# A fused attention, dense and expert kernel: another order of the work around the routing of tokens and between the two stages

## The chip, the cores and the metric

The kernel runs on one core of one Trainium2 chip. The metric is the device time of one execution in microseconds (us). Before the change the median of three runs is 1416.9 us (1415.62 to 1420.39). TensorE appears as PE, VectorE as DVE, ScalarE as ACT, GpSimd as POOL, and SyncE, which issues the transfers, as SP.

## What is computed

Attention in chunks of 64 gives x for 4608 tokens of 512 numbers. A dense layer with a parametric ReLU follows, and on its result a mixture of eight experts, of which each token takes one (cut from the reference):

```python
h = x @ w_in                                              # (4608, 2048)
g = np.maximum(h, 0.0) + alpha * np.minimum(h, 0.0)
x = g @ w_out                                             # (4608, 512)
logits = x @ w_gate                                       # 8 experts
expert_idx = np.argmax(logits, axis=1)
...
gate_w = probs[np.arange(N), expert_idx]                  # softmax weight of that expert
for e in range(E):
    mask = expert_idx == e
    out[mask] = gate_w[mask, None] * (np.maximum(x[mask] @ w1[e], 0.0) @ w2[e])   # 512 -> 1024 -> 512
```

## The kernel before

**Numbers.** Each float32 operand of a large matmul is split into a high and a low part, and three matmuls stand for one product. The high part is an ACT copy, the low part a subtraction, mostly on POOL.

**Dense stage.** The 36 tiles of 128 tokens go in 18 pairs j, each pair in 16 steps m of 128 hidden units, step s = 16 j + m in all. In a step TensorE does mm1 (12 matmuls, L328), ACT takes the positive and the negative part from PSUM (g_r, L344 and L345), DVE joins them with alpha (g_x, L350), ACT and POOL split the result (g_h L354, g_l L358), and TensorE accumulates mm2 (6 matmuls, L380) three steps behind mm1 into the banks y0 and y1, one for each tile of the pair. There are two buffers r, so the Relu of step s waits until g_l of step s - 2 has read its own. Every step also carries pieces of the attention of later tiles (exponentials px, their row sums sr, the product L269 on POOL, the transpose ptt L274 on DVE, matmuls L186 and L299) and of the split of the expert weights (ACT L467, POOL L468), which SP writes to HBM and later loads in blocks of 2 MB, the ring.

**Routing of a tile.** When a pair is done, gate_ev copies its two banks into rows (ACT L392), which sets y0 and y1 free for the next pair. Then gate_l makes eight dot products on DVE (L404), gate_a the largest logit and the one-hot tile oh (DVE L413 to L419), gate_e the exponential (ACT L425), gate_r the rank of each token among those of its expert (two small matmuls, L435 reading oh and L436 reading the running sum ohsum), gate_b weight, place and the new ohsum (DVE L450 to L458) and an indirect scatter of the row into the experts' table in HBM (POOL L459).

**Order.** It is written out by hand. The dictionaries pre and bg hold what a step does besides its own work; GATE (L558) sets the steps of a tile's routing, counted from the start of the pair behind its own: pieces of gate_l, then (a, r, b), the steps of gate_a, gate_r and gate_b. Even and odd tiles have different rows. Each engine works through its instructions in the order of the program:

```python
hooks(pre, s); g_b(*order[s - 1]); mm1(j, m); g_a(j, m); hooks(bg, s)
while done <= s - 3: mm2(*order[done]); done += 1
```

**Expert stage.** The expert tokens come in slots t of 128 rows. load gets them, with an address from a table, in transfers on SP's queue, tx transposes and splits them (blocks: DVE L661, ACT L663, POOL L664), m1(t, f) does 12 matmuls of 512 columns for one half f of the hidden units and 16 copies hx out of PSUM (ACT L692 or DVE L694), th(t, f) transposes and splits these, m2(t, f) does 12 matmuls more. Slots 0 to 3 (FULL is 4) use an expert that was picked before all counts were known; from slot 4 on addresses and weights come from tables that DVE computes from the counts of all tiles (table_count to table_refill). load_early fetches the second half of the ring, refill the blocks after it, under flags that table_refill writes. A value that SP or TensorE has to read holds up all that stands behind it on that queue.

**Between the stages** stands the tuple START (L885): the routing of the last two tiles a and b, the slots 0 to 3 and the tables, in one order by hand. It ends with tx(5) and table_refill, and the loop behind it goes over t from 3 on: tx(t + 2), m1(t + 1, 0), refill, m1(t + 1, 1), refill, th(t + 1), m2(t, 0), m2(t, 1), load(t + 4).

Of the kernel before, what the change touches and what calls it, by code (L numbers as in the profile page):

```python
# [42 lines left out]
def tile_attention_moe(ctx, tc, q, k, v, w_in, w_out, alpha, w_gate, w1, w2, out):  # L43
    nc = tc.nc
    NB = q.shape[0]
    NTILE = 2 * NB
    FULL = (NTILE - 4) // 8
    NT = 128 * NTILE
    MF = 16
# [7 lines left out]
    T = NTILE + 2 * (E - 1)  # L57
    TS = NTILE + 3
# [475 lines left out]
    def at(step, f, *args):  # L534
        bg.setdefault(step, []).append((f, args))
# [12 lines left out]
    for i in range(4):  # L548
        for d, e0, f in GATE0[i]:
# [12 lines left out]
    )  # L562
    for i in range(4, NTILE - 2):
        s0 = MF * (i // 2 + 1)
        pre.setdefault(s0 + 3, []).append((gate_ev, (i,)))
        *parts, (a, r, b) = GATE[2 if i % 2 and i >= NTILE - 5 else i % 2]
        for d, e0, e1 in parts:
            at(s0 + d, gate_l, i, e0, e1)
        at(s0 + a, gate_a, i)
        at(s0 + a + 1, gate_e, i)  # L570
        at(s0 + r, gate_r, i)
        pre.setdefault(s0 + b, []).append((gate_b, (i,)))
# [109 lines left out]
    def m1(t, f):  # L682
        if f == 0 and t >= FULL:
            half[t] = nc.tensor.value_load(rt[0:1, 0, t:t + 1], min_val=0, max_val=1)
        p = hbank("h", 3)
        passes(p, xT[t], f, t, True, True)
        hx[t, f] = P2["hx"].tile([128, 4, 128], F32, name="hx")
        for I in range(4):
            for J in range(4):
                src, dst = p[32 * I:32 * I + 32, 128 * J:128 * J + 128], hx[t, f][32 * J:32 * J + 32, I]  # L690
                if f == 0 or t < FULL:
                    nc.scalar.activation(out=dst, in_=src, func=ACTF.Relu)  # L692
                else:
# [185 lines left out]
    for t in range(3):  # L879
# [3 lines left out]
    at(B0 + 9, tx, 1)  # L883
    a, b = NTILE - 2, NTILE - 1
    START = (  # L885
        (mm2, NB - 1, MF - 1), (gate_ev, a), (gate_ev, b), (gate_l, a, 0, 4), (m1, 0, 0), (gate_l, a, 4, 8),
        (m1, 0, 1), (gate_a, a), (th, 0, 0), (gate_l, b, 0, 1), (gate_e, a),
        (m1, 1, 0), (th, 0, 1), (tx, 2), (gate_l, b, 1, 4), (gate_r, a), (m1, 1, 1), (th, 1, 0), (gate_b, a),
        (load_early, 1, 0), (gate_l, b, 4, 8), (gate_a, b), (gate_e, b), (m2, 0, 0), (load_early, 1, 1), (m2, 0, 1),
        (tx, 3), (m1, 2, 0), (th, 1, 1), (table_count,), (gate_r, b), (gate_b, b), (m1, 2, 1), (table_experts,),  # L890
        (th, 2, 0), (load_early, 1, 2), (m2, 1, 0), (table_places,), (table_own, 0, 8), (table_base, 0, 8), (load, 4),
        (load, 5), (m2, 1, 1), (th, 2, 1),
        (m1, 3, 0), (table_own, 8, T), (table_order,), (th, 3, 0), (tx, 4), (m1, 3, 1), (load_early, 1, 3), (th, 3, 1),
        (table_next,), (m2, 2, 0), (table_base, 8, T), (m2, 2, 1), (load, 6), (tx, 5), (table_refill,),
    )

    def hooks(d, s):
        for f, args in d.pop(s, []):
            f(*args)

    with tc.manual_schedule():
# [40 lines left out]
        mm2(j, m - 1)  # L942
        for f, *args in START:
            f(*args)
        for t in range(3, TS):
            more, two, dyn = t + 1 < TS, t + 2 < TS, t >= FULL
            if two and t > 3: tx(t + 2)
            if more: m1(t + 1, 0)
            if dyn: refill(t, 0)
            if more: m1(t + 1, 1)  # L950
            if dyn: refill(t, 1)
            if more:
                th(t + 1, 0)
# [66 lines left out]
```

## Time and profile before

| | |
|---|---|
| runs, median (lowest to highest) | 1416.9 us (1415.62 to 1420.39) |
| profiled execution, its own time | 1414.75 us |
| its span | 1412.9 us |
| mean granted TensorE clock | 0.989 |
| busy: PE, DVE, ACT, POOL | 1336.7, 1039.9, 825.5, 741.0 us |
| attention and dense stage | to about 950 us of the span |
| between the stages, up to m1(6, 0) | 949.80 to 1027.70 us |

A row of a timeline gives the start in us from the begin of the span, the length of the instruction (or of several, xN), engine, line, operation, output and inputs, and in brackets how long the engine sat idle before it and what ended that. Busy times of matmuls overlap a little, since they are pipelined.

### The profile page before, as it was taken

What the parts mean: (1) busy time and instruction counts of PE and PEld (TensorE: products, weight loads), DVE (VectorE), ACT (ScalarE), POOL (GpSimd) and SP (SyncE); (2) the same over time, 40 slices, a digit from 0 to 9 for tenths busy, and PEclk for the clock granted to TensorE, in tenths of its full rate; (3) what the DMA queues carried; (4) which work ended last, traced back from release to release, by engine and by line L of the source; (5) the groups of instructions that cost most, each with busy time, mean ns of one, the idle gap of its engine ahead of it and who ended that gap; (6) DMA issues with size and microseconds to landing.
All of it is one profiled execution on the core that took longest, in us unless ns stands there. A gap on an engine that the chain in (4) does not pass through costs nothing. (4 is left out here: it accounts for less than half of the span.)

```text
span 1412.9 us, 31146 instructions
## 1 busy us (share of the span) xinstructions
PE 1336.7 (95%) x9515; PEld 1155.7 (82%) x9515; DVE 1039.9 (74%) x2510; ACT 825.5 (58%) x2297; POOL 741.0 (52%) x754
## 2 busy tenths in 40 slices
PE   7788999999999999999999999998899999999997
PEld 6667888889888888988888898886688888878775
DVE  7996789788788778878877887567756556655553
ACT  4555555656556565655656565438565666556553
POOL 4553467665666666566666654333344444444443
PEclk9999999999999999999999999999999999999999
DMA  6645445655555555555555551191324415865543
GB/s 230 201 151 183 153 165 197 200 179 188 182 188 184 195 193 178 190 182 192 180 196 191 179 182 46 39 389 74 118 55 165 165 50 214 329 240 219 182 170 140
DMA packets 107306, 249.16 MB, mean 176 GB/s; under 512 B 15552, under 2 KB 36544, under 8 KB 103040
## 3 DMA queue, kind: packets, MB, share of 16 engines
q1 hardware_dynamic: 101136, 227.37, 47.6%
q0 software_dynamic: 6000, 19.70, 3.7%
q8 instruction: 84, 1.38, 0.4%
q14 instruction: 86, 0.70, 0.2%
HBM read 401.39 MB, written 88.91 MB: 347 GB/s over the span
## 5 line engine op out<-in xcount | busy, mean ns | idle before, releaser
L328 PEld LDWEIGHTS h<-xt,ring 128*128 128x128 f32 x3456 | 456.4, 193 | 40.3 <-DVE xt L315 4.0
L328 PE MATMUL h<-xt,ring 128*128 128x256 f32 x3456 | 466.1, 285 | 13.0 <-DVE xt L315 3.5
L380 PE MATMUL y<-ring,g 128*128 128x512 f32 x1728 | 457.0, 400 | 5.4 <-POOL g L358 3.0
L380 PEld LDWEIGHTS y<-ring,g 128*128 128x128 f32 x1728 | 307.1, 190 | 62.6 <-POOL g L358 4.7
L358 POOL TENSOR_TENSOR g<-r,g 128x256 fp32r<-128x256 f32 x281 | 248.4, 887 | 130.6 <-ACT g L354 113.4
L404 DVE CUSTOM_DVE_ANT_0 junk<-row,wgb 128x512 bf16<-128x512 f32 x288 | 268.9, 934 | 7.7 <-ACT row L392 3.6
L468 POOL TENSOR_TENSOR sp<-eraw,sp 128x512 fp32r<-128x512 f32 x128 | 177.9, 1390 | 162.2 <-ACT sp L467 136.4
L694 DVE TENSOR_SCALAR hx<-h 32x128 f32<-32x128 f32 x560 | 160.7, 287 | 104.6 <-PE h L676 97.4
L676 PE MATMUL y<-ring,hT 128*128 (+1 forms) x936 | 225.0, 395 | 10.4 <-ACT hT L663 7.2
L664 POOL TENSOR_TENSOR hT<-z,hT 128x512 fp32r<-128x512 f32 x78 | 100.2, 1303 | 253.4 <-ACT hT L663 250.2
L676 PE MATMUL h<-ring,xT 128*128 (+1 forms) x936 | 226.5, 396 | 5.2 <-DMA ring<-wsp 3.7
L676 PEld LDWEIGHTS y<-ring,hT 128*128 128x128 f32 x936 | 177.0, 190 | 52.7 <-ACT hT L663 9.3
L344 ACT ACTIVATE r<-h 128x256 f32<-128x256 f32 x288 | 110.3, 383 | 185.0 <-PE h L328 93.2
L676 PEld LDWEIGHTS h<-ring,xT 128*128 128x128 f32 x936 | 175.7, 188 | 48.9 <-ACT xT L663 4.0
L354 ACT ACTIVATE g<-r 128x256 fp32r<-128x256 f32 x288 | 119.3, 414 | 149.4 <-DVE r L350 79.3
L692 ACT ACTIVATE hx<-h 32x128 f32<-32x128 f32 x688 | 184.4, 268 | 10.6 <-PE h L676 3.0
L663 ACT ACTIVATE hT<-z 128x512 fp32r<-128x512 f32 x78 | 47.9, 633 | 123.6 <-DVE z L661 122.6
L257 ACT ACTIVATE px<-s 32x256 f32<-32x256 f32 x240 | 89.9, 375 | 4.1 <-DVE s L246 1.2
L467 ACT ACTIVATE sp<-eraw 128x512 fp32r<-128x512 f32 x128 | 80.8, 631 | 1.0
L661 DVE STREAM_TRANSPOSE z<-xg 128x512 f32<-128x512 f32 x39 | 27.7, 710 | 50.4 <-POOL hT L664 50.4
L661 DVE STREAM_TRANSPOSE z<-hx 128x512 f32<-128x512 f32 x78 | 51.3, 692 | 13.7 <-ACT hx L692 10.1
L664 POOL TENSOR_TENSOR xT<-z,xT 128x512 fp32r<-128x512 f32 x39 | 51.7, 1325 | 11.9 <-ACT xT L663 11.5
(734 smaller groups left out, 1192.9 us busy)
## 6 DMA issues: line engine op xcount, KB each, us to landing
ring<-wsp SPq DMA_DIRECT2D x148, 2048.0 KB
wsp<-sp SPq DMA_DIRECT2D x128, 512.0 KB
eraw<-in_w SPq DMA_DIRECT2D x128, 256.0 KB
xg<-xs SPq DMA_DIRECT2D x156, 64.0 KB
vt<-in_v SPq DMA_DIRECT2D x18, 512.0 KB
qt<-in_q SPq DMA_DIRECT2D x17, 512.0 KB
kt<-in_k SPq DMA_DIRECT2D x17, 512.0 KB
iraw<-in_w_in SPq DMA_DIRECT2D x16, 512.0 KB
```

What stands on the lines that cost most here:

```text
L257: nc.scalar.activation(out=p[J:J + 32, t], in_=s[I:I + 32, e], func=ACTF.Exp, scale=scale)
L328: nc.tensor.matmul(out=h, lhsT=w[:, wl, a, 128 * mi:128 * mi + 128], rhs=x[:, xl, a], start=(n == 0), stop=(n == 11),)
L344: nc.scalar.activation(out=r, in_=h, func=ACTF.Relu)
L354: nc.scalar.activation(out=gs[j, m][:, 0], in_=rs[j, m][0], func=ACTF.Copy)
L358: eng.tensor_tensor(out=g[:, 1], in0=r, in1=g[:, 0].bitcast(F32), op=ALU.subtract)
L380: nc.tensor.matmul(out=ys[j][t], lhsT=g[:, gl, 128 * t:128 * t + 128], rhs=w[:, wl, mi], start=(m == 0 and n == 0), stop=(m == MF - 1 and ...
L404: nc.vector.tensor_tensor_reduce(out=junk, in0=r[:, 0:512], in1=wgb[e // 2][:, e % 2], scale=1.0, scalar=0.0, op0=ALU.mult, op1=ALU.add, a ...
L468: eng.tensor_tensor(out=dst[:, 1], in0=raw, in1=dst[:, 0].bitcast(F32), op=ALU.subtract)
L664: nc.gpsimd.tensor_tensor(out=dst[:, 1], in0=z, in1=dst[:, 0].bitcast(F32), op=ALU.subtract)
L676: ins.append(nc.tensor.matmul(out=out, lhsT=lhs[:, xl, a], rhs=w[:, rows_, wl, a], start=(first and a == 0 and n == 0), stop=(last and a = ...
L692: nc.scalar.activation(out=dst, in_=src, func=ACTF.Relu)
L694: V.tensor_scalar(out=dst, in0=src, scalar1=0.0, scalar2=None, op0=ALU.max)
```

## The change

Three things. **GATE:** for tiles 4 to 29 the odd row's (a, r, b) goes from (16, 17, 18) to (17, 22, 24): gate_a one step later, the rank matmuls five steps behind it, gate_b two steps behind these. The even row's gate_b goes from step 15 to 16. Tiles 30 to 33 keep what they had. **hx:** the 16 copies of m1(3, 1) go from ACT to DVE (`t < FULL - 1`). **START:** rewritten, and extended to m2(4, 1); the loop begins at slot 5. In the new file, lines behind L563 have a number higher by one, and those behind START one lower by three.

```diff
     GATE = (
+        ((3, 0, 2), (4, 2, 3), (5, 3, 4), (6, 4, 6), (8, 6, 8), (9, 14, 16)),
+        ((10, 0, 2), (11, 2, 4), (12, 4, 5), (13, 5, 6), (14, 6, 8), (17, 22, 24)),
         ((3, 0, 2), (4, 2, 3), (5, 3, 4), (6, 4, 6), (8, 6, 8), (9, 14, 15)),
-        ((10, 0, 2), (11, 2, 4), (12, 4, 5), (13, 5, 6), (14, 6, 8), (16, 17, 18)),
         ((11, 0, 2), (12, 2, 5), (13, 5, 8), (13, 15, 16)),
     )
...
-        *parts, (a, r, b) = GATE[2 if i % 2 and i >= NTILE - 5 else i % 2]
+        *parts, (a, r, b) = GATE[i % 2 + (2 if i >= NTILE - 6 else 0)]
...
-                if f == 0 or t < FULL:
+                if f == 0 or t < FULL - 1:
...
-        (load_early, 1, 0), (gate_l, b, 4, 8), (gate_a, b), (gate_e, b), (m2, 0, 0), (load_early, 1, 1), (m2, 0, 1),
...
+        (m2, 0, 0), (load_early, 1, 1), (gate_r, b), (th, 1, 0), (table_count,), (table_experts,), (gate_e, b),
...
+        (table_base, 8, T), (m2, 3, 0), (th, 4, 1), (load, 7), (table_refill,), (m1, 5, 0), (refill, 4, 0), (load, 8),
+        (m2, 3, 1), (th, 5, 0), (m1, 5, 1), (refill, 4, 1), (m2, 4, 0), (th, 5, 1), (m2, 4, 1),
     )
+    FIRST = 5
...
-        for t in range(3, TS):
+        for t in range(FIRST, TS):
             more, two, dyn = t + 1 < TS, t + 2 < TS, t >= FULL
-            if two and t > 3: tx(t + 2)
+            if two: tx(t + 2)
```

TensorE in the dense stage, at the end of a pair (y_6936 and y_6937 are its banks). Before:

```order
L328 MATMUL h<-xt,ring_65 128x256 x12
L435 LDWEIGHTS tri
L435 MATMUL rk<-oh,tri 128x8
L436 LDWEIGHTS ones
L436 MATMUL rk<-ohsum,ones 128x8
L380 MATMUL y_6936<-ring_68,g 128x512 x3
L380 MATMUL y_6937<-ring_68,g 128x512 x3
L328 MATMUL h<-xt,ring_65 128x256 x12
L380 MATMUL y_6936<-ring_68,g 128x512 x3
L380 MATMUL y_6937<-ring_68,g 128x512 x3
L328 MATMUL h<-xt,ring_65 128x256 x12
```

The odd tile's rank matmuls (L435, L436) stand here two steps ahead of the pair's last mm2. After, at the begin of the next pair, whose banks are y_7625 and y_7626:

```order
L380 MATMUL y_7625<-ring_66,g 128x512 x3
L380 MATMUL y_7626<-ring_66,g 128x512 x3
L328 MATMUL h<-xt,ring_67 128x256 x12
L380 MATMUL y_7625<-ring_66,g 128x512 x3
L380 MATMUL y_7626<-ring_66,g 128x512 x3
L328 MATMUL h<-xt,ring_67 128x256 x12
L435 LDWEIGHTS tri
L435 MATMUL rk<-oh,tri 128x8
L436 LDWEIGHTS ones
L436 MATMUL rk<-ohsum,ones 128x8
L380 MATMUL y_7625<-ring_66,g 128x512 x3
L380 MATMUL y_7626<-ring_66,g 128x512 x3
```

Now the old pair closes without them, and they stand after the third mm2 of the new pair.

ACT at the same place, where the two L392 are the evictions of the pair's banks. Before:

```order
L344 ACTIVATE r<-h 128x256
L345 ACTIVATE n__7506<-h 128x256
L425 ACTIVATE lg,se<-lg 128x8
L467 ACTIVATE sp<-eraw 128x512
L354 ACTIVATE g<-r 128x256
L344 ACTIVATE r<-h 128x256
L345 ACTIVATE n__7554<-h 128x256
L392 ACTIVATE row<-y_6936 128x512
L392 ACTIVATE row<-y_6937 128x512
L354 ACTIVATE g<-r 128x256
```

After:

```order
L344 ACTIVATE r<-h 128x256
L345 ACTIVATE n__7496<-h 128x256
L467 ACTIVATE sp<-eraw 128x512
L354 ACTIVATE g<-r 128x256
L344 ACTIVATE r<-h 128x256
L345 ACTIVATE n__7541<-h 128x256
L425 ACTIVATE lg,se<-lg 128x8
L392 ACTIVATE row<-y_6924 128x512
L392 ACTIVATE row<-y_6925 128x512
L354 ACTIVATE g<-r 128x256
```

The exponential of the odd tile (L425) went behind the parts of one more step and is the last instruction ahead of the evictions.

POOL there (L459 is the scatter of a tile's rows, L269 the product of the attention). Before:

```order
L468 TENSOR_TENSOR sp<-eraw,sp 128x512
L459 DMA xs<-row,posi 36864x514
L358 TENSOR_TENSOR g<-r,g 128x256
L269 TENSOR_TENSOR px<-px,sr 128x512
L468 TENSOR_TENSOR sp<-eraw,sp 128x512
L358 TENSOR_TENSOR g<-r,g 128x256 x2
L468 TENSOR_TENSOR sp<-eraw,sp 128x512
L459 DMA xs<-row,posi 36864x514
L358 TENSOR_TENSOR g<-r,g 128x256
L393 COPY row<-toki 128x1 x2
```

After:

```order
L468 TENSOR_TENSOR sp<-eraw,sp 128x512
L358 TENSOR_TENSOR g<-r,g 128x256
L269 TENSOR_TENSOR px<-px,sr 128x512
L468 TENSOR_TENSOR sp<-eraw,sp 128x512
L459 DMA xs<-row,posi 36864x514
L358 TENSOR_TENSOR g<-r,g 128x256 x2
L468 TENSOR_TENSOR sp<-eraw,sp 128x512
L358 TENSOR_TENSOR g<-r,g 128x256
L393 COPY row<-toki 128x1 x2
L358 TENSOR_TENSOR g<-r,g 128x256
```

The even tile's scatter went from ahead of L269 to behind it and the split L468, ahead of the two g_l of steps 15 and 16; the odd tile's left this place for the next pair's steps.

TensorE between the stages, from m1(1, 1) on (h is an output of m1, y one of m2). Before:

```order
L676 MATMUL h<-ring_66,xT 128x512 x12
L676 MATMUL y<-ring_67,hT 128x512 x12
L676 MATMUL y<-ring_68,hT 128x512 x12
L676 MATMUL h<-ring_65,xT 128x512 x12
L725 LDWEIGHTS ones
L725 MATMUL cps<-ohsum,ones 128x8
L726 LDWEIGHTS ones
L726 MATMUL cps<-oh,ones 128x8
L435 LDWEIGHTS tri
L435 MATMUL rk<-oh,tri 128x8
L436 LDWEIGHTS ones
```

After:

```order
L677 MATMUL h<-ring_66,xT 128x512 x12
L677 MATMUL y<-ring_67,hT 128x512 x12
L435 LDWEIGHTS tri
L435 MATMUL rk<-oh,tri 128x8
L436 LDWEIGHTS ones
L436 MATMUL rk<-ohsum,ones 128x8
L726 LDWEIGHTS ones
L726 MATMUL cps<-ohsum,ones 128x8
L727 LDWEIGHTS ones
L727 MATMUL cps<-oh,ones 128x8
L677 MATMUL h<-ring_65,xT 128x512 x12
L677 MATMUL y<-ring_68,hT 128x512 x12
```

Between m2(0, 0) and m2(0, 1) stand now the last tile's rank, the count (L726, L727) and m1(2, 0); the rank stood behind m1(2, 0) and the count before it.

## Rows read from the trace of the kernel before

**Rows 1.** The page's part 1, the busy times of the engines.

```profile
PE 1336.7 (95%) x9515; PEld 1155.7 (82%) x9515; DVE 1039.9 (74%) x2510; ACT 825.5 (58%) x2297; POOL 741.0 (52%) x754
```

**Rows 2.** Waits of TensorE: released tile, releaser, total us, times, longest.

```profile
PE rk L435 <- DVE oh L418: 17.2, 13, 1.4
```

**Rows 3.** Timeline of TensorE, the end of one pair: start, length, operation, idle before.

```profile
596.28 1.59 PE L328 MATMUL h<-xt,ring 128*128 128x256 f32 x12
597.71 0.18 PE L435 MATMUL rk<-oh,tri 128*128 128x8 f16 x1
...
604.90 1.59 PE L328 MATMUL h<-xt,ring 128*128 128x256 f32 x12
607.82 0.17 PE L435 MATMUL rk<-oh,tri 128*128 128x8 f16 x1 [1.32 <-DVE oh L418]
...
614.77 1.43 PE L380 MATMUL y<-ring,g 128*128 128x512 f32 x5
```

**Rows 4.** Timeline of DVE, same stretch.

```profile
602.17 0.47 DVE L350 SCALAR_TENSOR_TENSOR r<-n__8127,nalpha,r 128x256 f32<-128x256 f32 x1
...
605.52 0.15 DVE L413 TENSOR_REDUCE gmx<-lg 128x1 f32<-128x8 f32 x1
...
607.68 0.77 DVE L419 TENSOR_SCALAR lg<-lg,gmx 128x8 f32<-128x8 f32 x1
...
610.25 0.11 DVE L450 TENSOR_SCALAR se<-se 128x1 f32<-128x1 f32 x1
```

**Rows 5.** Timeline of POOL, same stretch.

```profile
602.38 1.17 POOL L459 DMA_INDIRECT xs<-row,posi  x1 [0.15 <-ACT sp L467]
...
605.31 1.20 POOL L269 TENSOR_TENSOR px<-px,sr 128x512 f32<-128x512 f32 x1 [0.98 <-DVE sr L268]
606.47 1.26 POOL L468 TENSOR_TENSOR sp<-eraw,sp 128x512 fp32r<-128x512 f32 x1
607.70 1.43 POOL L358 TENSOR_TENSOR g<-r,g 128x256 fp32r<-128x256 f32 x2
```

**Rows 6.** Timeline of ACT, same stretch.

```profile
601.47 0.38 ACT L345 ACTIVATE n__8127<-h 128x256 f32<-128x256 f32 x1
...
608.46 0.39 ACT L344 ACTIVATE r<-h 128x256 f32<-128x256 f32 x1 [2.34 <-POOL g L358]
...
609.00 0.21 ACT L425 ACTIVATE lg<-lg 128x8 f32<-128x8 f32 x1
...
611.66 1.29 ACT L392 ACTIVATE row<-y 128x512 f32<-128x512 f32 x2
```

**Rows 7.** Timeline of DVE behind the dense stage: dot products and gate_a of tile a.

```profile
949.95 0.69 DVE L404 CUSTOM_DVE_ANT_0 junk<-row,wgb 128x512 bf16<-128x512 f32 x1 [3.58 <-ACT row L392]
...
955.84 0.16 DVE L413 TENSOR_REDUCE gmx<-lg 128x1 f32<-128x8 f32 x1
...
956.63 0.23 DVE L419 TENSOR_SCALAR lg<-lg,gmx 128x8 f32<-128x8 f32 x1
```

**Rows 8.** Timeline of TensorE between dense and expert stage.

```profile
962.49 0.73 PE L676 MATMUL y<-ring,hT 128*128 128x512 f32 x2 [1.18 <-ACT hT L663]
...
969.20 4.06 PE L676 MATMUL y<-ring,hT 128*128 128x512 f32 x10 [0.64 <-POOL hT L664]
...
1019.60 0.73 PE L676 MATMUL y<-ring,hT 128*128 x2 [3.53 <-ACT hT L663]
```

**Rows 9.** Windows: stretch, busy time of each engine (count), granted clock, DMA share.

```profile
949.80:1027.70 77.90, 67.50 (x271) 51.02 (x270) 59.03 (x184) 55.88 (x186) 25.93 (x21) 0.96 0.33 112
1027.70:1105.27 77.57, 77.57 (x338) 63.23 (x337) 45.90 (x133) 47.00 (x140) 34.22 (x28) 1.00 0.40 136
```

**Rows 10.** Groups of TensorE from 949.8 to 1027.7: busy, mean ns, idle before.

```profile
L676 PE MATMUL h<-ring,xT 128*128 128x512 f32 (+1 forms) x144 | 35.6, 399 | 1.5 <-POOL xT L664 1.5
L676 PE MATMUL y<-ring,hT 128*128 128x512 f32 (+1 forms) x120 | 33.2, 429 | 8.9 <-ACT hT L663 6.4 <-POOL hT L664 2.5
```

**Rows 11.** The page's part 5, the hx copies on DVE.

```profile
L694 DVE TENSOR_SCALAR hx<-h 32x128 f32<-32x128 f32 x560 | 160.7, 287 | 104.6 <-PE h L676 97.4
```

More of the change, by code (lines that the diff above doesn't have):

```diff
@@ L885, in tile_attention_moe @@
     START = (
-        (mm2, NB - 1, MF - 1), (gate_ev, a), (gate_ev, b), (gate_l, a, 0, 4), (m1, 0, 0), (gate_l, a, 4, 8),
-        (m1, 0, 1), (gate_a, a), (th, 0, 0), (gate_l, b, 0, 1), (gate_e, a),
-        (m1, 1, 0), (th, 0, 1), (tx, 2), (gate_l, b, 1, 4), (gate_r, a), (m1, 1, 1), (th, 1, 0), (gate_b, a),
-        (load_early, 1, 0), (gate_l, b, 4, 8), (gate_a, b), (gate_e, b), (m2, 0, 0), (load_early, 1, 1), (m2, 0, 1),
[L890 to L894, printed above, removed]
+        (mm2, NB - 1, MF - 1), (gate_ev, a), (gate_l, a, 0, 4), (gate_ev, b), (gate_l, a, 4, 8), (gate_l, b, 0, 1),
+        (gate_a, a), (m1, 0, 0), (m1, 0, 1), (th, 0, 0), (gate_e, a), (tx, 2), (gate_l, b, 1, 4), (gate_l, b, 4, 8),
+        (m1, 1, 0), (load_early, 1, 0), (gate_r, a), (gate_b, a), (gate_a, b), (th, 0, 1), (m1, 1, 1), (tx, 3),
+        (m2, 0, 0), (load_early, 1, 1), (gate_r, b), (th, 1, 0), (table_count,), (table_experts,), (gate_e, b),
+        (m1, 2, 0), (gate_b, b), (th, 1, 1), (m2, 0, 1), (load_early, 1, 2), (table_places,), (m1, 2, 1),
+        (load_early, 1, 3), (table_own, 0, 8), (table_base, 0, 8), (th, 2, 0), (table_own, 8, T), (th, 2, 1), (load, 4),
+        (tx, 4), (m1, 3, 0), (table_order,), (m2, 1, 0), (m1, 3, 1), (m2, 1, 1), (load, 5), (m2, 2, 0), (th, 3, 0),
+        (tx, 5), (m2, 2, 1), (table_next,), (load, 6), (th, 3, 1), (m1, 4, 0), (m1, 4, 1), (tx, 6), (th, 4, 0),
+        (table_base, 8, T), (m2, 3, 0), (th, 4, 1), (load, 7), (table_refill,), (m1, 5, 0), (refill, 4, 0), (load, 8),
+        (m2, 3, 1), (th, 5, 0), (m1, 5, 1), (refill, 4, 1), (m2, 4, 0), (th, 5, 1), (m2, 4, 1),
     )
+    FIRST = 5
     def hooks(d, s):
```

## The prediction

> **What bounds the kernel now.** I read four views in this order. First the page's busy times: TensorE works in 1336.7 of the span's 1412.9 us, 95% [rows 1], so a gain has to come out of the some 76 us in which it doesn't, and any other engine matters only where TensorE waits for it. Second, TensorE's waits: the longest entry is the rank matmul of a token tile waiting for its one-hot tile, 17.2 us in 13 waits [rows 2]. Third, the timeline of TensorE over the end of one pair of tiles, where that wait is seen twice: the even tile's rank matmul starts 1.43 us after the mm1 before it (596.28 to 597.71, no wait), the odd tile's 2.92 us after it (604.90 to 607.82) [rows 3]. Fourth, the stretch between dense and expert stage, 949.80 to 1027.70. It holds 264 expert matmuls (144 with output h, 120 with output y), ahead of which TensorE sat idle for 1.5 and 8.9 us [rows 10]. In the steady expert stage behind it 338 matmuls take 77.57 us, 0.2295 us each [rows 9].
>
> The profiled execution took 1414.75 us (span 1412.9); the sum is made against it. The median of the runs is 1416.9, 2.15 higher, and I add that at the end. About 0.3%, 4.3 us, is what a measurement of this kernel tells from no change.
>
> **The rank matmuls (GATE).** For 13 odd tiles the step of the rank matmul moves from one behind the one-hot tile to five behind it. A step is one mm1 and one mm2, close to 2.9 us, so the matmul comes some 14 us after the one-hot and cannot wait for it. Removed: 2.92 - 1.43 = 1.49 us per pair, 13 x 1.49 = 19.4 us (the waits alone, 17.2, leave out the refilling of the pipe). The 13 even tiles keep their rank matmul at step 14 and only move their bookkeeping and scatter by a step. Nothing is added: the same matmuls, DVE instructions and scatters are issued.
>
> What is late next? The one-hot piece (gate_a) of the odd tile is now one step later on DVE, and its exponential stands on ACT directly ahead of the two evictions that set the y banks free for the next pair. TensorE's first mm2 of that pair began at 614.77 [rows 3] and now wants its bank 1.49 earlier, at 613.28. I follow the chain to the eviction with the old durations:
> - ACT's negative part of step 15 starts at 601.47 and takes 0.38 [rows 6], so DVE's g_x can start at about 601.85. It stood at 602.17 behind the even tile's gate_b [rows 4], which has gone from there, so everything from it to POOL's px moves 0.3 earlier: px from 605.31 [rows 5] to 605.0.
> - POOL then does px (1.16 to the next start), the split sp (1.23), and now the even tile's scatter, which stood ahead of px at 602.38: 1.35 with the gap before it. Then g_l of step 15, 0.72, half of the pair at 607.70 [rows 5]. It will end at 609.5 (605.0 + 1.16 + 1.23 + 1.35 + 0.72), where it ends at 608.4 now.
> - ACT's Relu of step 17 waits for exactly that (608.46, after 2.34 us idle) [rows 6]. From there over the negative part, DVE's g_x and the transpose ptt to the next DVE instruction at 610.25 [rows 4] are 1.79 us, so gate_a starts at about 611.3.
> - gate_a costs 1.0 us undisturbed (955.84 to 956.86) [rows 7] and 2.9 at this place now (605.52 to 608.45) [rows 4]. Then 0.2 for the exponential and 0.64 for one eviction [rows 6]. So y0 comes free between 613.1 and 615.0: margin from +0.1 to -1.8 us.
>
> The difference is what POOL does meanwhile. At 605.5 POOL ran a split and two g_l back to back; at 611.3 I expect the end of a split and one g_l, so one held instruction and not three: 1.0 + 0.5 (half of a POOL instruction of 0.72 to 1.3 us) = 1.5. That frees the bank at 613.64, 0.36 late; 13 x 0.36 = 4.7 us. **Dense stage: 4.7 - 19.4 = -14.7 us**, with ends -19.4 (no new wait) and 13 x 1.76 - 19.4 = +3.5 (a new wait of 1.76 each time).
>
> That DVE's small instructions stretch beside POOL is in the rows: the same lg instruction takes 0.23 in one place and 0.77 in the other [rows 4, 7]. The Trainium skill, "SBUF — State Buffer", section "Who interferes with whom", says that DVE and GpSimd share one port pair under an exclusive lock, and that a DVE instruction with two SBUF inputs is held by a GpSimd instruction that reads SBUF until that has ended. By that rule gate_a's cost depends on where POOL's instructions fall, and a placement like today's gives the +3.5 end, a sum of -8; by my reading of POOL's order it is -14.7.
>
> **The transition (START).** 264 x 0.2295 = 60.6 us of matmuls stand in 77.9, so 17.3 us are lost there: 10.4 idle [rows 10], about 0.04 x 67.5 = 2.7 from a granted clock that averages 0.96 where the steady stage has 1.00 [rows 9] (of the two levels, 1.2 and 2.4 GHz, it shows the lower in part of it, behind waits), the remaining 4.2 refilling after each wait. In the new order other blocks stand between a transpose and its reader. I go through the waits:
> - m2(0,0) still comes right behind m1(1,1), four blocks after the start, and th(0,0) still stands behind 32 hx copies on ACT. The wait stays: 1.18 for ACT and about 0.64 for POOL [rows 8], 1.8. If the clock falls behind it, ten matmuls that need 2.3 at full pace took 4.06 [rows 8], up to 1.8 more; I take 1.0.
> - m2(0,1) gets m1(2,0) ahead of it (12 x 0.23 = 2.8) and m2(1,1) gets m1(3,1): their waits go. m2(4,0) waited 3.53 [rows 8], because hx(4,1) stood behind the whole of table_refill on DVE. Now it stands ahead of it, and m2(3,0), m1(5,0), m2(3,1), m1(5,1), 11 us, lie between m1(4,1) and m2(4,0). Gone, with the slow clock behind it.
> - New: the last tile's rank matmul stands right behind m2(0,0), at 949.8 + 60 x 0.23 + 1.8 = 965.4 or a little later. Its one-hot on DVE: 16 dot products at 0.74 (949.95 to 955.84 for eight [rows 7]), two gate_a at 1.0, and two transposes and a gate_b, 0.7 each by their lengths in this stretch: 15.9 in all, 965.8. From 0 to 2.3 (with one gate_a at 2.9 instead of 1.0); I take 1.0. Its matmuls and the count's hold everything behind them on TensorE.
> - New: m1(6,0) waits for refill(4,0) on SP's queue, which waits for the flags at the end of table_refill. DVE had 59.0 us of work in the stretch [rows 9], of which about 6 come behind the flags; 16 hx copies of slot 3 come to it (16 x 0.287 = 4.6) [rows 11]. About 58 of the 66 us that would be left: free if DVE idles under 8 us before that. It idled 18.9 in the whole stretch now. From 0 to 3; I take 0.5. SP's skipped transfers themselves cost nothing that TensorE sees.
> - The 16 copies leave ACT, which is not last there any more; on DVE m2(1,1) and m2(2,0), 5.5 us, cover their 4.6. All ring loads of half 1 go ahead of load(4) now; what a late xT costs TensorE is 1.5 us in the whole stretch now [rows 10]: nothing taken, half of it at the upper end.
> - Refilling: I leave two fifths of the 4.2, 1.7, for the first wait and the two that can be new.
>
> What stays is 1.8 + 1.0 + 1.0 + 0.5 + 1.7 = 6.0: **transition 17.3 - 6.0 = -11.3 us**. Ends: -14.7, where only the first wait and half of that refilling stay (1.8 + 0.8 = 2.6 of 17.3), and -5.9, where everything stands at its upper end (1.8 + 1.8 + 2.3 + 3 + 1.7 + 0.8 = 11.4).
>
> **Sum.** -14.7 - 11.3 = -26 us: 1388.75 on the profiled execution, 1390.9 against the median. I say 1391. The slots behind m2(4,1) are the same as before and steady.
>
> **Rivals.**
> - *Nothing takes the place.* For it: the bank's margin is +0.1 with an undisturbed gate_a, and DVE and POOL may run earlier than I chain them. Against it: every number of the chain would have to be at its low end. -19.4 - 14.7 = -34.1: 1382.8. Chance 0.14.
> - *The eviction waits at its far end.* gate_a is held as long as now, in all 13 pairs: dense +3.5, transition -11.3, together -8: 1409; half way, 1401. For it: the 2.9 at today's place [rows 4]. Against it: POOL's order behind that g_l is lighter there. 0.14, for times from 1401 to 1413.
> - *Slower, by the same bank.* If one more POOL split (1.23) gets ahead of g_l of step 15, the bank comes 1.76 + 1.23 = 2.99 late: 13 x (2.99 - 1.49) = +19.5 in the dense stage, less 11.3, +8: 1425. For it: POOL has a split in most steps, and one that is issued a step early blocks g_l for its whole length [rows 5]. Against it: the new order of POOL shows none there. It decides from 1.49 + 11.3 / 13 = 2.36 us late, 0.6 beyond the far end of my chain. 0.04.
> - *The change doesn't do what it says*: a rank matmul could still wait, now for the sum of one-hots (ohsum) that the even tile's later gate_b writes. Against it: that gate_b stands ahead of the odd tile's gate_a on DVE, so it is done five steps before as well. Then only the transition gains, 1405.6, or with its waits moved to loads behind SP's queue nothing, 1417. Together 0.06.
>
> **How the numbers follow.** My forecast, a gain of 16 to 32 us, has 0.62, times from 1385 to 1401. The time I give is its sum, 1391. The range 1382 to 1406 takes in the first rival and the lower half of the second, and leaves out some 0.17. Faster by over 0.3%: 0.62 + 0.14 + 0.13 + 0.03 = 0.92; within 0.3%: 0.04; slower: 0.04.
>
> **What would show it.** The waits of TensorE should have no "rk <- DVE oh" of 13 times any more; a new entry of a dense y (L380) waiting for an ACT row (L392) with 13 times and 0.2 to 0.6 us each is my term of 4.7, about none the first rival, 1.8 each the second. Between the first m1(0,0) and m1(6,0) should lie about 66.6 us, with the wait of m2(0,0) unchanged, none for hT of slot 4, and at most 1 to 2 us for the last rank matmul. I am wrong in the mechanism if the dense stage gains less than 8 us without that y wait, or if the transition gains under 6.

## The result, and the profile after

The changed kernel takes 1400.05 us (median of four runs, 1399.02 to 1401.04), the kernel before beside it 1418.64 (1415.62 to 1421.03): a ratio of 0.987, 95% interval 0.9846 to 0.9894. The forecast was faster, 1391 us, in a range from 1382 to 1406. The direction and the range held; the time lies 9 us above the forecast, and the profile shows that this is not noise but a step of the working.

The profiled execution took 1399.97 us, its span is 1398.2, 14.7 less than before. Four places of it answer to the rows above. First the waits of TensorE over the whole span (released tile, releaser, total us, times, longest), the two longest and the one for the flags, and then the one for the ring in the kernel before:

```profile
PE h L677 <- DMA ring<-wsp: 8.0, 5, 3.3
PE rk L435 <- DVE xt L315: 6.7, 13, 3.2
...
PE h L677 <- DVE cm L853: 1.5, 1, 1.5
```

```profile
PE h L676 <- DMA ring<-wsp: 3.7, 3, 1.6
```

The 17.2 us for the one-hot tile [rows 2] are gone. In their place the rank matmul waits for xt, the DVE instruction that reads the attention's product o (one of the 13 waits, 3.2 us, is in the kernel before as well), and the waits for the ring are now the largest entry.

Second, TensorE at an even tile's rank matmul (590.40, step 14 as before), at the first mm2 of the next pair (605.83), and at the odd tile's rank matmul (614.39), which stands behind the third mm2 of that pair, against [rows 3]:

```profile
588.53 1.59 PE L328 MATMUL h<-xt,ring 128*128 128x256 f32 x12
590.40 0.18 PE L435 MATMUL rk<-oh,tri 128*128 128x8 f16 x1 [0.28 <-DVE xt L315]
...
605.83 1.66 PE L380 MATMUL y<-ring,g 128*128 128x512 f32 x6
...
612.96 1.59 PE L328 MATMUL h<-xt,ring 128*128 128x256 f32 x12
614.39 0.18 PE L435 MATMUL rk<-oh,tri 128*128 128x8 f16 x1
```

The odd tile's matmul follows its mm1 at 1.43 us, where it was 2.92: all of the 1.49 is gone. But the even tile's, which was not moved, now follows its mm1 at 1.87 us with a wait, where it was 1.43 without one. So 0.44 a pair have come in at a place that the change doesn't name.

Third, the stretch between the stages. It was 77.90 us from the first m1 to m1(6,0) [rows 9]; now:

```profile
936.10 8.56 PE L677 MATMUL h<-ring,xT 128*128 128x512 f32 x36
...
948.79 0.73 PE L677 MATMUL y<-ring,hT 128*128 128x512 f32 x2 [1.18 <-ACT hT L664]
950.52 2.58 PE L677 MATMUL y<-ring,hT 128*128 128x512 f32 x10 [1.00 <-POOL hT L665]
953.05 0.17 PE L435 MATMUL rk<-oh,tri 128*128 128x8 f16 x1
...
1004.08 3.04 PE L677 MATMUL h<-ring,xT 128*128 x12 [1.50 <-DVE cm L853]
1008.70 3.03 PE L677 MATMUL h<-ring,xT 128*128 x12 [1.59 <-DMA ring<-wsp]
```

That is 67.98 us, 9.9 less. The wait of 3.53 for slot 4 [rows 8] is gone, the first m2 waits as before, the last rank matmul doesn't wait. But m1(6,0) waits 1.50 for the flags (cm, L853, is the last part of table_refill), and m1(6,1) 1.59 for its ring.

Fourth, the expert stage. At m1(6,0) the kernel is 23.6 us ahead (1027.70 against 1004.08), at its end 14.7. The rows of TensorE's timeline with a wait for the ring, behind 1010 us:

```profile
1230.78 5.46 PE L677 MATMUL h<-ring,xT 128*128 x12 [3.25 <-DMA ring<-wsp]
1236.46 3.11 PE L677 MATMUL h<-ring,xT 128*128 x12 [0.22 <-DMA ring<-wsp]
...
1294.29 4.57 PE L677 MATMUL h<-ring,xT 128*128 x12 [2.19 <-DMA ring<-wsp]
...
1352.11 3.03 PE L677 MATMUL h<-ring,xT 128*128 x12 [0.72 <-DMA ring<-wsp]
```

The block of 1230.78 takes 5.46 us where 3.04 is usual. So 8.9 us were given back: 1.9 at m1(6,1) (m2(5,0) comes 21.73 earlier, no longer 23.6), and the rest at these ring loads, with the slow clock behind them. From the first m1 to the end of the span it is 463.1 us before and 462.1 now: **of what the new order between the stages gained, 1 us is left.**

The queue that posts the ring loads is SP's. Its wait for the flags between the stages (930 to 1006 us) now, and the same entry before (943 to 1030):

```profile
SPq L857 <- DVE cm L853: 15.2, 1, 15.2
```

```profile
SPq L856 <- DVE cm L852: 5.0, 1, 5.0
```

SP stands 15.2 us at the flags where it stood 5.0. It posts its first refill at 1003.85, 67.8 us behind the first m1; before it was at 1013.08, 63.3 us behind the first m1. TensorE came 9.9 us earlier to m1(6,0), and SP's queue, counted from the same point, began 4.5 us later.

How long is that queue? SP posts the row loads (L645) of one slot per turn. From those of slot 8 to those of slot 38 it is 1004.83 to 1342.07 us, 30 turns of 11.24 us, where TensorE's turn without a wait is 11.07 (m1 at 1028.10 and 1039.17). SP's waits for earlier ring loads in these turns (1004.8 to 1342 us), at a refill (L861) and at the small load gi (L648):

```profile
SPq L861 <- DMA ring<-wsp: 39.5, 11, 5.2
SPq L648 <- DMA ring<-wsp: 6.9, 5, 2.1
```

They are 46.4 us, 1.55 of each turn. Without them a turn would be shorter than TensorE's; with them it is a little longer.

### The profile page after: what moved, and what is told of

Same layout as the page of the kernel before. It is cut to its first block, busy times and chain, and to the rows that moved or that the text cites. A ratio compares the mean times of both kernels' runs of the same rounds, so it can differ in the third digit from the quotient of the medians.

```text
span 1398.2 us, 31107 instructions
## 1 busy us (share of the span) xinstructions
PE 1337.1 (96%) x9515; PEld 1156.5 (83%) x9515; DVE 1035.7 (74%) x2526; ACT 816.4 (58%) x2281; POOL 729.2 (52%) x754
## 5 line engine op out<-in xcount | busy, mean ns | idle before, releaser
L358 POOL TENSOR_TENSOR g<-r,g 128x256 fp32r<-128x256 f32 x281 | 242.0, 864 | 159.4 <-ACT g L354 143.6
L404 DVE CUSTOM_DVE_ANT_0 junk<-row,wgb 128x512 bf16<-128x512 f32 x288 | 289.9, 1007 | 7.8 <-ACT row L392 3.6
L695 DVE TENSOR_SCALAR hx<-h 32x128 f32<-32x128 f32 x576 | 165.4, 287 | 109.1 <-PE h L677 101.7
L468 POOL TENSOR_TENSOR sp<-eraw,sp 128x512 fp32r<-128x512 f32 x128 | 173.5, 1355 | 130.7 <-ACT sp L467 107.2
L677 PE MATMUL h<-ring,xT 128*128 (+1 forms) x936 | 230.3, 401 | 9.5 <-DMA ring<-wsp 8.0
L677 PE MATMUL y<-ring,hT 128*128 (+1 forms) x936 | 221.5, 391 | 4.9 <-POOL hT L665 2.9
L693 ACT ACTIVATE hx<-h 32x128 f32<-32x128 f32 x672 | 180.1, 268 | 15.8 <-PE h L677 8.3
```

Source lines behind the costliest of these rows:

```text
L358: eng.tensor_tensor(out=g[:, 1], in0=r, in1=g[:, 0].bitcast(F32), op=ALU.subtract)
L404: nc.vector.tensor_tensor_reduce(out=junk, in0=r[:, 0:512], in1=wgb[e // 2][:, e % 2], scale=1.0, scalar=0.0, op0=ALU.mult, op1=ALU.add, a ...
L468: eng.tensor_tensor(out=dst[:, 1], in0=raw, in1=dst[:, 0].bitcast(F32), op=ALU.subtract)
L677: ins.append(nc.tensor.matmul(out=out, lhsT=lhs[:, xl, a], rhs=w[:, rows_, wl, a], start=(first and a == 0 and n == 0), stop=(last and a = ...
```

## The experiments

The theory (A): in the expert stage SP's queue has about as much to do as TensorE, starts at the flags, and so takes back what TensorE gains over it. The rival (B): the ring's transfers themselves, their bytes, set the pace, and whoever comes earlier waits. In the dense part: the 0.44 a pair is a wait for the PSUM pair that the rank matmul shares with the attention's o, and goes if the odd tile's rank matmul comes a step later.

### One part at a time

`gate_only` is the kernel before with the new GATE and the line that picks from it:

```diff
+        ((3, 0, 2), (4, 2, 3), (5, 3, 4), (6, 4, 6), (8, 6, 8), (9, 14, 16)),
+        ((10, 0, 2), (11, 2, 4), (12, 4, 5), (13, 5, 6), (14, 6, 8), (17, 22, 24)),
...
-        ((10, 0, 2), (11, 2, 4), (12, 4, 5), (13, 5, 6), (14, 6, 8), (16, 17, 18)),
...
-        *parts, (a, r, b) = GATE[2 if i % 2 and i >= NTILE - 5 else i % 2]
+        *parts, (a, r, b) = GATE[i % 2 + (2 if i >= NTILE - 6 else 0)]
```

> The GATE part alone; order between the stages and hx copies as in the kernel before. Theory A (flags): the dense stage of the changed kernel ended 13.7 us earlier (949.80 to 936.10), and the tables for the expert stage move with it, so nothing is given back: 13 to 14 us faster than before, TensorE's waits for the ring as before (3.7 us, 3 waits), 12 waits of a rank matmul for xt of some 0.28 us. Rival B (transfers): the ring loads limit the expert stage whenever TensorE comes to it early; then part of the 13.7 is lost there again, waits for the ring over 6 us, 5 to 9 us faster than before.

Measured: 1406.92 us (1403.07 to 1407.36), ratio 0.9925 (0.9905 to 0.9945), some 11 us faster. The first m1 stands at 935.88, 13.9 earlier, and the waits for xt are there, 6.7 in 13 (one of them, 3.2, is in the kernel before as well). From the first m1 to the end it is 465.3 us, 2.2 more than before, with ring waits of 4.6. This lies between the two expectations: it shows what the dense part is worth, and doesn't tell A from B.

`start_only` is the changed kernel with just these lines as they were, so with everything else of the change.

> START, FIRST and the hx copies alone; GATE as before. Theory A (flags): m1(6,0) comes 9.9 us earlier (67.98 in place of 77.90 us from the first m1), but the flags of table_refill come nearly as late as before, counted from the first m1 (67.9 where it was 63.4 us), so SP loses its lead and 8.9 us are lost in the expert stage: 0 to 3 us faster than before, waits for the ring 7 to 9 us. Rival B (the two parts add up and the loss belongs to GATE): about 9.9 us faster, waits for the ring as before.

Measured: 1414.31 (median of ten, 1412.88 to 1418.20), ratio 0.998 (0.9968 to 0.9991), 1.3 to 4.5 us faster. m1(6,0) comes 67.9 us behind the first m1, as in the changed kernel, ring waits are 10.7 us, and from the first m1 to the end it is 463.8. So the loss belongs to START: it gains 10 us and keeps about 3. What takes it back, these two don't say.

### The rank matmul one step later

```diff
-        ((10, 0, 2), (11, 2, 4), (12, 4, 5), (13, 5, 6), (14, 6, 8), (17, 22, 24)),
+        ((10, 0, 2), (11, 2, 4), (12, 4, 5), (13, 5, 6), (14, 6, 8), (17, 23, 25)),
```

> The changed kernel with the odd row's (a, r, b) as (17, 23, 25): rank and gate_b one step later still. Theory (PSUM bank): the rank matmul shares the PSUM pair with the attention's product o, and waits for DVE to read o (xt, L315); 12 waits of 0.28 us, each with a rank step of 1.87 in place of 1.43 us behind its mm1, 0.44. One step later the bank is read: these waits go, 12 x 0.44 = 5.3 us faster than the changed kernel, 1394.8. Rival 1 (another wait takes the place, of the dense y for the evicted row, or of o for the rank's reader): 0 to 2 us faster. Rival 2 (the waits cost nothing that matters, lost again in the expert stage): no change, waits for the ring up by as much.

Measured: 1395.88 us (1395.47 to 1398.36), 4.2 less than the changed kernel. TensorE's waits from 230 to 930 us, first of the changed kernel, then of this one:

```profile
PE rk L435 <- DVE xt L315: 3.4, 12, 0.4
...
PE y L380 <- ACT row L392: 0.2, 1, 0.2
```

```profile
PE rk L435 <- DVE pos L455: 0.8, 2, 0.7
```

The twelve waits are gone and no other came in the dense stage. From the third rank matmul of the run to the first m1 it is 725.6 us in the changed kernel (210.52 to 936.10) and 720.2 here (212.18 to 932.41): 5.35 us, the 12 x 0.44 expected. Of these 4.2 are left in the median: behind the first m1 this kernel takes 464.2 us, 2.1 more, with ring waits of 10.8 us.

The number is the expected one, its reason is not. In code gate_r does take its tile from the pair of banks that also holds o, but the matmul that waited is the even tile's, and this edit doesn't move it. What it moves is the odd tile's rank matmul, which never waited, and the odd tile's gate_b. DVE, first in the changed kernel (even tile's mm1 at 588.53), then here (587.62):

```profile
572.84 0.10 DVE L450 TENSOR_SCALAR se<-se 128x1 f32<-128x1 f32 x1
...
575.11 3.53 DVE L404 CUSTOM_DVE_ANT_0 junk<-row,wgb 128x512 bf16<-128x512 f32 x1
...
589.67 0.68 DVE L315 TENSOR_TENSOR xt<-o,xt 128x512 fp32r<-128x512 f32 x1
```

```profile
573.85 1.10 DVE L404 CUSTOM_DVE_ANT_0 junk<-row,wgb 128x512 bf16<-128x512 f32 x1
...
574.89 0.14 DVE L450 TENSOR_SCALAR se<-se 128x1 f32<-128x1 f32 x1
...
588.06 0.68 DVE L315 TENSOR_TENSOR xt<-o,xt 128x512 fp32r<-128x512 f32 x1
```

In the changed kernel gate_b (from L450 on) stands ahead of two dot products (L404), and the second of them takes 3.53 us; here it stands behind them, and they take 1.54 and 1.10. So xt ends 1.82 us behind the start of the even tile's mm1 there, later than the 1.43 at which the rank matmul could start, and 1.12 here, as in the kernel before (597.40 against 596.28). That gate_b's place is the cause is read from these rows; no run moves it alone. POOL worked without a gap from 575.40 to 578.08 beside the long dot product; that this held it is not shown.

`rank_alone` puts two of the three moves in GATE back:

```diff
-        ((3, 0, 2), (4, 2, 3), (5, 3, 4), (6, 4, 6), (8, 6, 8), (9, 14, 16)),
+        ((3, 0, 2), (4, 2, 3), (5, 3, 4), (6, 4, 6), (8, 6, 8), (9, 14, 15)),
...
-        ((10, 0, 2), (11, 2, 4), (12, 4, 5), (13, 5, 6), (14, 6, 8), (17, 23, 25)),
+        ((10, 0, 2), (11, 2, 4), (12, 4, 5), (13, 5, 6), (14, 6, 8), (16, 23, 25)),
```

> The kernel with rank 23 with the one-hot piece back at step 16 and the even tile's gate_b back at 15, so that of the dense part only the rank matmul and what hangs on it (odd gate_b) is late: (9, 14, 15) and (16, 23, 25). If the late rank alone is the gain, 1395.9 again within 2 us. If the other two moves are needed, since DVE or POOL are late at the pair's end (the y banks, the attention's sums), a wait shows up there and it is 3 to 15 us slower.

Measured: 1396.84 us (1395.03 to 1398.86) beside 1395.88, and no new wait of TensorE in the dense stage. The odd tile's late rank and gate_b alone are the gain; the one-hot's and the even tile's steps could have stayed.

### The flags and SP's queue

`hx_act` leaves all hx copies up to slot 4 to ACT:

```diff
-                if f == 0 or t < FULL - 1:
+                if f == 0 or t < FULL + 1:
```

> The changed kernel with the 32 hx copies of m1(3,1) and m1(4,1) both on ACT. Theory A (flags): DVE has 9.6 us less to do ahead of table_refill's flags, they come at about 994 in place of 1004, SP gets its lead back: the wait of m1(6,0) for the flags (1.5) and of m1(6,1) for its ring (1.6) go and the ring waits of the expert stage fall from 6.4 to 2 to 4 us; 6 to 9 us faster than the changed kernel, 1391 to 1394. Rival B (transfers limit, whatever SP does): the first two waits go and come back in the expert stage, 0 to 2 us faster. Rival C: ACT becomes last and m2(3,1) or m2(4,1) waits for its hT, 2 to 5 us slower.

Measured: 1402.90 us (1401.47 to 1403.49), 2.9 slower than the changed kernel. That is C's size, but not its place: m2(4,0) waited 1.9 us for its hT, m2(3,1) and m2(4,1) did not. The edit took 9.3 us from DVE, but the flags came no earlier. The timeline of DVE says why:

```profile
993.47 0.71 DVE L662 STREAM_TRANSPOSE z<-hx 128x512 f32<-128x512 f32 x1 [3.89 <-ACT hx L693]
...
999.91 0.71 DVE L662 STREAM_TRANSPOSE z<-hx 128x512 f32<-128x512 f32 x1 [3.56 <-POOL xT L665]
1000.54 0.11 DVE L844 TENSOR_REDUCE mo<-pos 1x1 f32<-1x8 f32 x1
```

The transposes of slot 4 stand ahead of table_refill on DVE and wait there, 3.89 us for ACT and 3.56 for POOL. SP posted its first refill 69.3 us behind the first m1, 1.6 later than in the changed kernel, and ring waits were 11.0. It is no test of A by its removal, only a small one by a delay: flags later, kernel slower.

`flags_early` keeps this edit and adds an order in which nothing stands ahead of the flags but their inputs:

```diff
-        (tx, 4), (m1, 3, 0), (table_order,), (m2, 1, 0), (m1, 3, 1), (m2, 1, 1), (load, 5), (m2, 2, 0), (th, 3, 0),
-        (tx, 5), (m2, 2, 1), (table_next,), (load, 6), (th, 3, 1), (m1, 4, 0), (m1, 4, 1), (tx, 6), (th, 4, 0),
-        (table_base, 8, T), (m2, 3, 0), (th, 4, 1), (load, 7), (table_refill,), (m1, 5, 0), (refill, 4, 0), (load, 8),
+        (tx, 4), (m1, 3, 0), (table_order,), (m2, 1, 0), (m1, 3, 1), (table_next,), (m2, 1, 1), (load, 5), (m2, 2, 0),
+        (th, 3, 0), (tx, 5), (m2, 2, 1), (table_base, 8, T), (load, 6), (th, 3, 1), (m1, 4, 0), (m1, 4, 1),
+        (table_refill,), (th, 4, 0), (tx, 6), (m2, 3, 0), (th, 4, 1), (load, 7), (m1, 5, 0), (refill, 4, 0), (load, 8),
```

> The changed kernel with START in another order once more: table_next, table_base(8, T) and table_refill stand as early on DVE as their inputs allow, and the hx copies of m1(3,1) and m1(4,1) are on ACT, so nothing of them stands ahead of the flags. Theory A (SP's queue starts at the flags and has as much work in the expert stage as TensorE): the flags come at about 57 us behind the first m1 in place of 67.8, m1(6,0) comes at 64 to 66 us without its waits, SP's refills 8 to 10 us earlier throughout, and the stage from the first m1 to the end, 462 to 465 us in all six kernels so far, falls to 453 to 457; 6 to 10 us faster than the changed kernel, 1390 to 1394. Rival B (the transfers themselves set the pace from the first real refill on): m1(6,0) comes as early, but the ring waits behind it grow by as much, 460 us or more from the first m1, 0 to 3 us faster.

Measured: 1395.24 us (1392.64 to 1395.76), 4.8 less than the changed kernel. SP's first refill came 57.9 us behind the first m1, as meant, and from the first m1 to the end it is 455.5 us, 6.6 less. The ring waits that are left:

```profile
1231.22 3.04 PE L677 MATMUL h<-ring,xT 128*128 x12 [0.98 <-DMA ring<-wsp]
...
1289.30 4.45 PE L677 MATMUL h<-ring,xT 128*128 x12 [2.50 <-DMA ring<-wsp]
...
1346.94 3.03 PE L677 MATMUL h<-ring,xT 128*128 x12 [0.66 <-DMA ring<-wsp]
```

SP's last group of refills stood 416.0 us behind the first m1 and stands at 409.3: of the 9.8 us that its queue began earlier, 6.7 arrive. The profiled execution gains less than the stage, 5.1 us, because its first part was longer (the third rank matmul at 212.1 in place of 210.5). The time from the first m1 lies in A's 453 to 457 and not in B's 460; the whole lies a little above A's 1394.

With rank 23 as well:

> Both together: the flags early and the odd row's (a, r, b) as (17, 23, 25). Theory A: both gains add, 1395.9 less 6 to 10, 1386 to 1390. Rival B: 1393 to 1396.

Measured: 1389.33 us (1388.02 to 1389.41), as A had it.

The test of SP itself, by more work and by less. `sp_more`:

```diff
         new.append(nc.sync.dma_start(out=gi[t], in_=src[:, 512:514]))
+        if 9 <= t < TS:
+            for z in range(2):
+                nc.sync.dma_start(out=P2["gi"].tile([1, 16], F32, name=f"gx{z}"), in_=alpha[0:1, 0:16])
```

> The changed kernel with two further transfers of 64 bytes a slot on SP's queue, from slot 9 on, whose data nobody reads: 60 instructions more on that queue, almost no bytes. Theory A (SP's queue is as long as TensorE's work): each costs it some 0.1 to 0.5 us, and its refills come later by 6 to 30 us at the end: at least 4 us slower, ring waits over 10 us. Rival B (the transfers or TensorE set the pace, SP has room): within 2 us of the changed kernel.

Measured: 1442.18 us (1440.84 to 1446.86), **42 us slower**, for under 4 KB. Waits of TensorE for the ring, and SP's waits for earlier ring loads in its 30 turns (1006 to 1383 us):

```profile
PE h L680 <- DMA ring<-wsp: 22.7, 10, 5.8
PE y L680 <- DMA ring<-wsp: 6.7, 4, 2.8
```

```profile
SPq L651 <- DMA ring<-wsp: 39.8, 10, 6.2
SPq L864 <- DMA ring<-wsp: 14.8, 5, 3.2
SPq L648 <- DMA ring<-wsp: 4.2, 5, 1.3
```

SP's turn is 12.59 us (1006.04 to 1383.87), 1.35 more than in the changed kernel. Most of that is the queue's own work: where nothing is held, groups of skipped refills follow each other at 10.2 to 10.6 us, and at 9.1 to 9.4 in the changed kernel. L651 is the added transfer. It too is held at its issue until an earlier ring load has landed, and the queue behind it with it, but these waits stand for the most part in place of those at the refills: all three rows are 58.8 us against 46.4, 0.41 more a turn.

`gi_pool` goes the other way, on the kernel with rank 23 and the late flags. What it does moves one small transfer a slot to POOL's queue:

```diff
-        new.append(nc.sync.dma_start(out=gi[t], in_=src[:, 512:514]))
+        row = nc.gpsimd.value_load(at_, min_val=0, max_val=(E * NTILE - 1) * 128)
+        new.append(nc.gpsimd.dma_start(out=gi[t], in_=xs[bass.ds(row, 128)][:, 512:514]))
```

> The kernel with rank 23 (flags as late as in the changed kernel, 1395.9), with the small transfer gi of each slot on POOL's queue in place of SP's. Theory A (SP's queue is the pace of the expert stage): it takes about 0.6 us a slot from SP (1026.73 to 1027.34 in the changed kernel's queue), 19 us over 31 slots, more than what can be gained: the ring waits of 10.8 us fall to under 4 although the flags come no earlier, and the kernel is 4 to 10 us faster, 1386 to 1392. Rival B (late flags or the transfers alone count): ring waits stay over 8 us, 0 to 2 us faster. Rival C (POOL's value read and transfer hold up its splits of hT): waits of y for POOL hT appear in each slot, slower.

Measured: 1384.99 us (1384.70 to 1385.47), ratio to the kernel before 0.976 (0.9733 to 0.9787), 10.9 less than rank 23 and a little more than expected. TensorE's waits at m1(6,0) and m1(6,1):

```profile
1001.83 3.03 PE L678 MATMUL h<-ring,xT 128*128 x12 [1.51 <-DVE cm L854]
1005.87 3.04 PE L678 MATMUL h<-ring,xT 128*128 x12 [1.00 <-DMA ring<-wsp]
```

The flags are as late as they were. But from 1010 us to the last slot there is no wait at all, and from the first m1 to the end it is 450.0 us. SP's turn is 10.60 us (1002.59 to 1320.49), now shorter than TensorE's. Its largest waits in these turns (1002.5 to 1320 us) are for ring loads, 11.0 us less than in the changed kernel, and for a row buffer that DVE still reads:

```profile
SPq L862 <- DMA ring<-wsp: 35.4, 12, 4.6
SPq L645 <- DVE z L663: 6.2, 7, 2.0
```

The same window of both kernels, the changed one first, then a stretch of the changed kernel alone (busy times of PE, PEld, DVE, ACT, POOL, then granted clock, DMA share and GB/s):

```profile
1100.00:1300.00 200.00, 194.33 (x824) 157.09 (x823) 113.44 (x327) 117.14 (x350) 83.55 (x69) 0.97 0.54 194
```

```profile
1100.00:1300.00 200.00, 200.00 (x869) 162.99 (x868) 119.74 (x346) 121.40 (x360) 98.69 (x90) 1.00 0.60 216
```

```profile
1210.00:1235.00 25.00, 21.75 (x86) 17.30 (x86) 13.22 (x38) 12.42 (x36) 10.93 (x9) 0.90 1.02 377
```

The DMA engines move more bytes in that time, not fewer. So B as stated, that whoever comes earlier waits, is out: the same loads allow a stage 12 us shorter when the queue posts them sooner. But the transfers have room only on the average. In the 25 us around the longest ring wait (1230.78) the DMA engines are full, share 1.02, and part of SP's turn is itself a wait for ring loads to land (1.55 us of 11.24, in gi_pool 1.18 of 10.60). What sets the pace is the queue, with these waits in it.

> The same with the flags early as well, beside 1389.3 with gi on SP. Theory A: ring waits nearly gone, 2 to 6 us faster, 1383 to 1387; both cures work on the same lead of SP, so their gains don't add in full. Rival B: no change.

Measured: 1384.69 us (1383.12 to 1385.66), and 450.3 us from the first m1: 4.6 less than flags_rank23, as A had it, and no gain over gi_pool. The waits at m1(6,0) and m1(6,1) are gone, but two between the stages came in their place (0.54 and 1.94 us ahead of m2(3,0), the ten matmuls behind it in 4.02 us); early flags are worth something only while SP is the pace.

Last, what START is worth then: rank 23 and gi on POOL with the old START, loop and hx copies.

> What START is worth when SP is not the pace: rank 23 and gi on POOL, with START, the loop and the hx copies of the kernel before, beside 1385.0 with the new START. Theory A: from the first m1 to m1(6,0) the old order takes 77.9 us, the new one 68.3 and then 1.3 for a late ring, and nothing behind them levels it: 8.3 us slower, 1393. Rival B (the late flags of the new order cost as much as it gains, SP or no SP): within 2 us, 1385.

Measured: 1392.31 us (1390.63 to 1393.20), 7.3 more than with the new START. From the first m1 to the end it is 458.2 against 450.0. The order's gain is real, 7 to 8 us of the 9.9, once SP can follow.

| kernel | median us | SP's first refill, us behind the first m1 | first m1 to end, us |
|---|---|---|---|
| before | 1418.64 | 63.3 | 463.1 |
| gate_only | 1406.92 | 63.3 | 465.3 |
| start_only | 1414.31 | 67.7 | 463.8 |
| changed | 1400.05 | 67.8 | 462.1 |
| hx_act | 1402.90 | 69.3 | 463.8 |
| rank23 | 1395.88 | 67.7 | 464.2 |
| rank_alone | 1396.84 | 67.8 | 464.0 |
| flags_early | 1395.24 | 57.9 | 455.5 |
| flags_rank23 | 1389.33 | 57.9 | 455.2 |
| sp_more | 1442.18 | 67.7 | 501.5 |
| gi_pool | 1384.99 | 68.1 | 450.0 |
| gi_pool_flags | 1384.69 | 58.0 | 450.3 |
| gi_pool_old_start | 1392.31 | 63.9 | 458.2 |

The last column is from one profiled execution each; the seven kernels with SP's queue as it was and the flags at 63 or later stand within 3.2 us of each other, whatever the order between the stages.

## Why the prediction was right, and where it was not

**The rank matmuls, -14.7 forecast.** The first m1 comes 13.7 us earlier. The removal (19.4) holds: rank 23, which waits for nothing, gives the missing 5.35, 19.05 with the 13.7. The size of what took its place, 4.7, was nearly right, and its mechanism wrong. The step that failed is "The 13 even tiles keep their rank matmul at step 14 and only move their bookkeeping and scatter by a step. Nothing is added". It put the even tiles at nothing, and their rank matmuls now wait for xt, 12 x 0.44 = 5.3 us, since DVE comes later to it. "What is late next?" followed the moved one-hot and exponential to the y bank, and not the moved gate_b to the next matmul that had little to spare: 0.31 us before, from xt's end at 597.40 to the matmul at 597.71. The y bank cost 0.2 us once. That 5.3 and 4.7 are so near each other is luck.

**The chain to the y bank** came out nearly as worked out. gate_a started 3.0 us ahead of the first mm2 of the next pair, where 2.0 were forecast, and took 1.7, where 1.5 were. DVE and POOL there:

```profile
602.85 0.12 DVE L413 TENSOR_REDUCE gmx<-lg 128x1 f32<-128x8 f32 x1
603.01 0.69 DVE L416 SCALAR_TENSOR_TENSOR key<-lg,gmx,desc 128x8 f32<-128x8 f32 x1
...
603.93 0.47 DVE L418 TENSOR_SCALAR oh<-key,km 128x8 f16<-128x8 f32 x1
```

```profile
602.37 1.30 POOL L468 TENSOR_TENSOR sp<-eraw,sp 128x512 fp32r<-128x512 f32 x1 [0.65 <-POOL g L358]
603.63 0.74 POOL L358 TENSOR_TENSOR g<-r,g 128x256 fp32r<-128x256 f32 x1
```

The instruction key, 0.23 us alone, ends at 603.70, as POOL's split does (603.67); oh ends at 604.40, as g_l does (604.37). For key, which reads two tiles, this is the lock of the Trainium skill, "SBUF — State Buffer", section "Who interferes with whom", in this trace. The rule's way to a sum of -8, a placement of POOL like the old one, did not come about.

**The transition, -11.3 forecast.** To m1(6,0) it gained 9.9. What stays was put at 6.0 and is 67.98 - 60.6 = 7.4: the first m2 as forecast, nothing for the last rank matmul (1.0), nothing for the clock behind the first m2 (1.0), 1.5 for the flags (0.5), the rest refilling and short waits.

**The step that failed** is one sentence behind the sum: "The slots behind m2(4,1) are the same as before and steady." I took the 77.57 us of [rows 9], without a wait, for the whole stage, and left the ring waits of 3.7 us at its end unread. They were the sign that SP was just keeping up. Of the refill I wrote that SP's skipped transfers "cost nothing that TensorE sees". With the loads, and with SP's waits for ring loads, a turn of its queue takes 11.24 us where TensorE's takes 11.07, and with the lead gone this showed 20 slots later. I had bounded the wait for the flags at m1(6,0) alone, 0 to 3, and not what they start. So -26 became -14.8 in the profiled execution: dense 13.7, between the stages 9.9, behind them +8.9.

The rival with the waits of the transition "moved to loads behind SP's queue" was on the list, at a few chances in a hundred, joined to a failure of the dense part. It should have stood alone, with SP's queue counted like an engine.

## What to carry to other kernels

Count the queue that posts the transfers like an engine: its time per turn of the loop, what it waits for, and when it starts; a reorder that brings the other engines forward is lost if that queue's first input (here flags from a table) doesn't come forward too. Where it is full, take transfers from it before anything else is reordered: the Trainium skill, "DMA: Bandwidth & Descriptors", section "Rules for kernel authors", says that spreading transfers over issuing engines gives no bandwidth and only saves issue time, and here one small transfer a slot less on SP's queue, with its issue and its waits, was worth 10.9 us. And when work is moved, follow each engine that it stands on, at its new place, to the next wait that had little to spare: an instruction that was not moved can begin to wait.

## What the runs showed of the hardware

- Transfers of 64 bytes on SP's queue cost 0.7 us each of the kernel's time (42 us for 60). They lengthen the queue's turn by 1.35 us for two; 0.41 of it are longer waits at issue for ring loads of 2 MB that have not landed.
- SP's issue is not short: four row loads take 1.90 us, a group of four refills that transfer nothing 3.54 us, and with the register reads a turn in which nothing is held comes to 9.1 to 9.4 us. With the waits for ring loads the mean turn is 11.24, where TensorE needs 11.07:

```profile
1020.46 3.54 SPq L861 DMA_DIRECT2D ring<-wsp  x4
1024.83 1.90 SPq L645 DMA_DIRECT2D xg<-xs  x4
1026.99 0.35 SPq L648 DMA_DIRECT2D gi<-xs  x1
1029.55 3.54 SPq L861 DMA_DIRECT2D ring<-wsp  x4
```

- A ring wait costs more than itself: behind one of 3.25 us the next twelve matmuls took 5.46 us in place of 3.04. The granted clock between 1210 and 1235 us was 0.90, in the stretch from 1180 to 1210 ahead of it 1.00; of the two levels, 1.2 and 2.4 GHz, that is the lower one for a part of it, from the wait on (0.50 between 1230 and 1235). Behind one of 0.72 us they took 3.03.

The fastest version, gi on POOL's queue with rank 23, with or without early flags, takes 1385 us, 15 less than the changed kernel. Why a transfer on SP is held until an earlier one has landed, by the hardware's queue or by the semaphores that the program's scheduler shares between transfers, was not tried and stays open.
